# Query softmax halves and weight residuals moved from VectorE to GpSimd, key maxima written as pairwise maxima, and key maxima and stores placed later

## The chip, the cores and the metric

The kernel runs on one core of one Trainium2 chip. The metric is the time of one execution on the device in microseconds (us). The kernel before was run three times: 1423.19 us is the median, 1422.28 the lowest and 1428.6 the highest.

Names of engines in the profile: PE is TensorE's matmul, PEld its weight load, DVE is VectorE, ACT is ScalarE, POOL is GpSimd, SP is SyncE. SPq, ACTq and so on are the sequencers of those engines, which issue DMAs and waits.

## What is computed

Three layers in a row, all on 4608 tokens of width 512, with the inputs q and k scaled up. First an attention with separate softmaxes, per batch (8) and head (8), sequence 576, head width 64:

```python
q_s = softmax(q, axis=-1)        # each query over its 64 columns
k_s = softmax(k, axis=2)         # each key column over the 576 positions
kv = einsum('bhsd,bhse->bhde', k_s, v)
x = einsum('bhsd,bhde->bhse', q_s, kv)
```

Its output, as rows of 512, goes through `leaky(x @ w_in) @ w_out` (512 to 2048 to 512, slope 0.01) and then through `max(x @ w1, x @ w2, x @ w3) @ w_out` (512 to 768 to 512). The weights are 64-bit floats, the rest is 32-bit. The kernel keeps every operand of the large products as a high and a low part and adds three products (high by high, high by low, low by high).

## The kernel before, in words

**Chunks and blocks.** The 4608 tokens are 9 chunks of 512. The first layer's weights are 16 blocks `m` of 128 columns, each with its part of `w_in` and of `w_out`. A step of the first stage takes one block for one chunk: `project` (12 matmuls of 512 columns, line 622), ACT's leaky activation (L899), the split of the result into `ghi` (ACT, L642) and `glo` (DVE, L643), and, one step later, `a_out` (12 matmuls). The list `TURNS` says which chunk takes which blocks: chunks 0 and 1 take turns while the weights still arrive, 32 steps in all, then chunk 2 takes all 16 blocks in steps 32 to 47. Chunks 3 to 8 go in three pairs through a seven-product scheme of half-size blocks (L849), and the last layer follows in the same manner for eight chunks and plainly for one.

**The opening.** For chunks 0 and 1 the attention is done before their first step. `q_unit` takes a maximum over groups of 64 (L521, DVE), subtracts it (L531, DVE), takes the exponential (L532, ACT), sums (L534, DVE), and multiplies by the reciprocal (L540, DVE); PE transposes the result (L546) and multiplies it by the key-value product (L554). `kv_unit` for these two blocks takes the key maxima through PE transposes (L409, L414 to L434) and multiplies keys by values on PE (L450).

**Conversion of a weight block.** `conv_a` and `split_words` turn a block of 64-bit words into the high and low parts: ACT copies one element of the newest `g` into the work tile `ca` (L171, which ties the conversion to a step) and takes absolute values (L172); DVE does five integer and scaling operations (L173, L174, L175, L178, L179), adds (L184), and subtracts the high part, which ACT has written meanwhile (L177), to leave the low part (L185); ACT copies the sum (L188) and its queue stores it (L189) for later use. The work tile `ca` has one buffer, so a conversion begins when the one before has let go of it. `BEGUN` gives the step at which each block's conversion is written: blocks 3 to 7 at steps 2, 3, 5, 7 and 9.

**Background units.** `background(step)` is called once a step, from step 28 to 47 twice a step, and three times in each round of a pair of chunks (each live unit advances by one `yield` a call). It advances `kv_unit` and `q_unit` of later chunks, `stage_a` (stores of a converted block, SP's queue, L679 to L686), and `sums_a` (loads two stored blocks, L694, forms sums and their parts, L230 to L239, and stores them, L705, SP's queue). For blocks from 2 on, `kv_unit` fetches keys on POOL's queue (L396), takes the key maxima on DVE (L438), has POOL take the maximum over partitions (L439), subtracts (L442), takes the exponential (L443) and multiplies (L450). `behind_step` ties the maximum to the newest `g` (L372). `post()` at the start of `background` runs what the list `posted` holds, or counts it down by one call.

**What sets the order.** The order in which each engine takes its instructions is fixed when the program is built: a scheduler orders them by readiness and by their place in the program; `pin` keeps an instruction behind everything already written for its engine. At run time each engine takes its instructions in that order.

Of the kernel before, what the change touches and what calls it, by code (L numbers as in the profile page):

```python
# [18 lines left out]
P = 128  # L19
# [20 lines left out]
AHEAD = 3  # L40

BEGUN = (0, 0, 0, 2, 3, 5, 7, 9, 11, 13, 15, 17, 19, 21, 23, 25)

# [28 lines left out]
def tile_kernel(ctx: ExitStack, tc: tile.TileContext, q, k, v, wa, wb, out):  # L72
# [82 lines left out]
    def split_words(raw, hi, lo, n, after=None, whole=None, keep=None):  # L155
# [24 lines left out]
        if whole is not None:  # L180
            af, bf = (t.rearrange("p (b n) -> p b n", n=H) for t in (af, bf))
            nc.vector.tensor_tensor(whole, af, bf, op=ALU.add)
            return
        nc.vector.tensor_tensor(af, af, bf, op=ALU.add)  # L184
        nc.vector.tensor_tensor(lo, af, hi.bitcast(F32), op=ALU.subtract)  # L185
        if keep is not None:
            copy = raw.bitcast(F32)[:, :N]
            nc.scalar.activation(copy, af[:, :N], AF.Copy)  # L188
            pin(nc.scalar.dma_start(keep, copy))  # L189

# [191 lines left out]
    def kv_unit(b, hp, early):  # L382
# [15 lines left out]
        if b < FIRST:  # L398
            nc.sync.dma_start(vt, v[b, hp])
        yield  # L400
        if b < FIRST:

# [32 lines left out]
        else:  # L435
            mx = ap.tile([P, P], F32, tag="mx", name="mx", bufs=2)
            behind_step(mx[:, 0:1])
            nc.vector.tensor_reduce(mx, ke.rearrange("p r d -> p d r"), axis=AX.X, op=ALU.max)  # L438
            nc.gpsimd.partition_all_reduce(mx, mx, P, bass_isa.ReduceOp.max)  # L439
# [3 lines left out]
            nc.scalar.activation(ke, ke, AF.Exp)  # L443
            yield
        yield
# [49 lines left out]
    def q_unit(c, hp, early):  # L495
# [28 lines left out]
        if by_scalar:  # L524
            for g in range(G):
                nc.scalar.activation(
                    groups[:, g], groups[:, g], AF.Exp, bias=mx[:, g : g + 1], accum_out=sm[:, g : g + 1]
                )
            yield
        else:  # L530
            nc.vector.tensor_tensor(groups, groups, mx[:, :, None].to_broadcast([P, G, W]), op=ALU.subtract)  # L531
            nc.scalar.activation(qt, qt, AF.Exp)  # L532
            yield
            nc.vector.tensor_reduce(sm, groups, axis=AX.X, op=ALU.add)  # L534
# [4 lines left out]
        nc.vector.reciprocal(sm, sm)  # L539
        nc.vector.tensor_tensor(groups, groups, sm[:, :, None].to_broadcast([P, G, W]), op=ALU.mult)  # L540
        yield
# [147 lines left out]
    def sums_a(t):  # L689
# [9 lines left out]
        hi, lo = split_sums(room)  # L699
        yield  # L700
        i = t * len(AUSES)
        for h, z in enumerate((hi, lo)):
# [49 lines left out]
    def ahead_units():  # L752
        for m in range(MA):
            yield max(BEGUN[m] + 5, 8), stage_a(m)
        for t in range(MA // 2):
            yield (30, 34, 38, 42, 49, 53, 57, 61)[t], sums_a(t)
        for u, at in enumerate((68, 78, 88, 98, 107, 112, 115, 119, 123)):
# [600 lines left out]
```

## Time and profile before

| what | value |
|---|---|
| median of three runs | 1423.19 us (1422.28 to 1428.6) |
| the profiled execution's own time | 1424.57 us |
| its span, first to last instruction | 1422.8 us |
| mean granted TensorE clock | 0.995 |
| PE busy | 1388.7 us, 98% of the span |
| DVE busy | 874.5 us, 61% |
| ACT busy | 673.8 us, 47% |
| POOL busy | 159.9 us, 11% |

How to read it: the span is the profiled execution alone, from the first instruction to the last; its own time lies 1.77 us above the span and 1.38 us above the median of the runs. Busy time of an engine is the time in which at least one of its instructions ran; PE's matmuls are pipelined, so a busy PE is not PE at its peak.

### The profile page before, as it was taken

The numbers are of one execution on the slowest core, as the hardware profiler recorded it, in microseconds if no ns is written. First come the engines' busy times: TensorE is split into PE (matmuls) and PEld (weight loads), VectorE is DVE, ScalarE is ACT, GpSimd is POOL, SyncE is SP. The second block draws the span as 40 slices with busy tenths as digits, with TensorE's granted clock in tenths as the row PEclk, the third lists the DMA queues.
The fourth block names the chain that finished last, engine by engine and source line by source line (L and its number), as shares of the span: only waits on it lengthen the run. The fifth ranks groups of instructions, "written<-read, shape, count | busy, mean of one in ns | idle before, by whom it ended". The sixth has DMA issues, their size and how long they took to land.

```text
span 1422.8 us, 18234 instructions
## 1 busy us (share of the span) xinstructions
PE 1388.7 (98%) x6624; PEld 1130.2 (79%) x6624; DVE 874.5 (61%) x1428; ACT 673.8 (47%) x1382; POOL 159.9 (11%) x261
## 2 busy tenths in 40 slices
PE   6999999999999999999999999999999999999998
PEld 5688877788788787888887888888888888888887
DVE  8888978875686794665755636767357345434311
ACT  6756867663666654654544444334124223323211
POOL 1000212200111120210122310101000000000000
PEclk9999999999999999999999999999999999999999
DMA  9468776734877856769589897764574573464611
GB/s 372 158 246 293 260 249 204 237 124 151 326 258 274 348 178 227 258 237 359 201 312 318 308 360 267 255 232 172 187 293 166 200 283 131 140 245 155 223 36 38
DMA packets 90825, 330.09 MB, mean 232 GB/s; under 512 B 10672, under 2 KB 27056, under 8 KB 67568
## 3 DMA queue, kind: packets, MB, share of 16 engines
q1 hardware_dynamic: 68512, 251.46, 48.5%
q0 software_dynamic: 19056, 66.98, 14.0%
q10 hardware_dynamic: 3168, 10.49, 1.8%
q8 instruction: 52, 0.85, 0.2%
q14 instruction: 37, 0.30, 0.1%
HBM read 253.66 MB, written 75.24 MB: 231 GB/s over the span
## 4 chain that ended last, share of the span: by engine, by line
PE 80%; DVE 7%; DMA 5%; issue 3%; ACT 3%; POOL 0%; SPq 0%; DVEq 0%; ACTq 0%; POOLq 0%
PE ps L849 37%; PE acc L622 30%; PE ps L622 11%; DMA stream<-room 2%; PE ps L450 1%; PE ps L574 1%; DMA room<-wi 1%; DVE glo L643 1%; DMA stream_in<-room 1%; DMA spare<-in_q_dram 1%; DVE qmx L521 0%; DMA ke<-in_k_dram 0%; DMA room<-in_wb_dram 0%; DMA qt<-in_q_dram 0%; DVE side L814 0%
## 5 line engine op out<-in xcount | busy, mean ns | idle before, releaser
L849 PE MATMUL ps<-op,group 128*128 128x512 f32 x1512 | 352.2, 389 | 0.0
L849 PEld LDWEIGHTS ps<-op,group 128*128 128x128 f32 x1512 | 283.7, 188 | 59.1 <-ACT snap L1081 0.2
L622 PE MATMUL acc<-ghi,outw 128*128 128x512 f32 x768 | 250.9, 394 | 3.6 <-ACT ghi L642 3.2
L849 PE MATMUL ps<-opA,group 128*128 128x512 f32 x1008 | 249.7, 391 | 1.4 <-ACT snap L977 1.2
L849 PEld LDWEIGHTS ps<-opA,group 128*128 128x128 f32 x1008 | 188.4, 188 | 41.9 <-ACT snap L977 2.0
L622 PEld LDWEIGHTS acc<-ghi,outw 128*128 128x128 f32 x768 | 144.3, 189 | 35.6 <-ACT ghi L642 5.2
L622 PE MATMUL acc<-glo,outw 128*128 128x512 f32 x384 | 151.6, 395 | 3.7 <-DVE glo L643 3.4
L622 PE MATMUL acc<-wo,h 128*128 128x512 f32 x558 | 135.6, 389 | 0.0
L622 PE MATMUL acc<-ghi,w 128*128 128x512 f32 x384 | 127.3, 395 | 0.0
L622 PE MATMUL ps<-xhi,w 128*128 128x512 f32 x384 | 125.8, 394 | 1.2 <-ACT g L899 0.8
L1081 ACT ACTIVATE snap<-ps 128x512 f32<-128x512 f32 x108 | 61.9, 596 | 136.0 <-PE ps L849 135.7
L622 PEld LDWEIGHTS acc<-wo,h 128*128 128x128 f32 x558 | 104.7, 188 | 21.7
L1096 DVE TENSOR_TENSOR snap<-snap,ps 128x512 f32<-128x512 f32 x72 | 49.1, 684 | 93.6 <-ACT snap L1081 70.3
L643 DVE TENSOR_TENSOR glo<-g,ghi 128x512 fp32r<-128x512 f32 x102 | 69.4, 687 | 46.8 <-ACT ghi L642 46.4
L622 PEld LDWEIGHTS acc<-glo,outw 128*128 128x128 f32 x384 | 72.5, 189 | 21.4 <-DVE glo L643 6.4
L622 PEld LDWEIGHTS ps<-xhi,w 128*128 128x128 f32 x384 | 72.0, 188 | 17.7 <-ACT g L899 1.2
L642 ACT ACTIVATE ghi<-g 128x512 fp32r<-128x512 f32 x102 | 63.5, 630 | 44.2 <-DVE g L1281 27.3
L622 PEld LDWEIGHTS acc<-ghi,w 128*128 128x128 f32 x384 | 71.5, 188 | 15.8 <-ACT ghi L642 0.4
L1092 DVE TENSOR_TENSOR best<-snap,ps 128x512 f32<-128x512 f32 x36 | 24.7, 686 | 87.9 <-PE ps L849 39.1
L622 PE MATMUL acc<-glo,w 128*128 128x512 f32 x192 | 75.9, 395 | 1.8 <-DVE glo L643 1.8
L622 PE MATMUL ps<-xlo,w 128*128 128x512 f32 x192 | 75.2, 392 | 0.1
L1105 ACT ACTIVATE h<-best 128x512 fp32r<-128x512 f32 x48 | 30.3, 631 | 86.7 <-DVE best L1098 86.2
(184 smaller groups left out, 1925.3 us busy)
## 6 DMA issues: line engine op xcount, KB each, us to landing
group<-stream SPq DMA_DIRECT2D x62, 1024.0 KB, 6.6
outw<-stream_out SPq DMA_DIRECT2D x48, 1024.0 KB, 7.7
group<-stream_in SPq DMA_DIRECT2D x42, 1024.0 KB, 7.4
stream<-room POOLq DMA_DIRECT2D x66, 256.0 KB, 6.5
raw<-in_wa_dram SPq DMA_DIRECT2D x16, 1024.0 KB, 7.6
x<-st SPq DMA_DIRECT2D x40, 256.0 KB, 3.6
room<-in_wb_dram POOLq DMA_DIRECT2D x18, 512.0 KB, 5.7
stream_out<-w SPq DMA_DIRECT2D x16, 512.0 KB, 3.5
```

The costliest lines, as they stand in the source:

```text
L450: nc.tensor.matmul(acc[z, : D + 1], lhsT=ke[:, r, z], rhs=vt[:, r, h], start=r == 0, stop=r == RK - 1)
L574: nc.tensor.matmul(both(xps, c0, c1), lhsT=a, rhs=halves(y, c0, c1), start=i == 0, stop=i == 2)
L622: nc.tensor.matmul(acc, lhsT=l, rhs=r, start=first and i == 0, stop=last and i == 2)
L642: nc.scalar.activation(hi[:, z], g[:, z], AF.Copy)
L643: nc.vector.tensor_tensor(lo[:, z], g[:, z], hi[:, z].bitcast(F32), op=ALU.subtract)
L849: nc.tensor.matmul(bank, lhsT=l, rhs=r, start=fresh and first, stop=last, skip_group_check=not fresh)
L1081: nc.scalar.activation(t, bank, AF.Copy)
L1092: nc.vector.tensor_tensor(g, snap, bank, op=ALU.add)
L1096: nc.vector.tensor_tensor(snap, snap, bank, op=ALU.add)
L1105: nc.scalar.activation(h[:, m, 0], g, AF.Copy)
```

## The change: what it does, and the diff

- In `split_words`, for weight blocks 3 to 7 (those with `FIRST < len(tiles) < FIRST_MAXIMUM`), the addition of L184 runs on GpSimd, and the last part (the subtraction of L185, pinned, ACT's copy L188 and the store L189) is posted and written one step later.
- In `kv_unit` the key maxima of L438 become four `tensor_tensor` maxima of 128x128 blocks in a row.
- In `kv_unit` for blocks 5 to 7 the maxima come one background call later; a `yield` behind the exponential goes, so that the product stays at its call.
- In `q_unit` of chunks 0 and 1 the subtraction (L531) and the multiplication (L540) run on GpSimd.
- In `sums_a` the stores come one call later, and the last four of the eight units begin one step earlier. `stage_a` begins two steps later, though not before step 8.

```diff
--- before.py
+++ after.py
@@ -39,6 +39,7 @@
 PARTS = ("a11", "a12", "a21", "a22", "s2", "s4", "s1", "s3")
 AHEAD = 3
 
+FIRST_MAXIMUM = 8
 BEGUN = (0, 0, 0, 2, 3, 5, 7, 9, 11, 13, 15, 17, 19, 21, 23, 25)
 
 
@@ -181,12 +182,22 @@
             af, bf = (t.rearrange("p (b n) -> p b n", n=H) for t in (af, bf))
             nc.vector.tensor_tensor(whole, af, bf, op=ALU.add)
             return
-        nc.vector.tensor_tensor(af, af, bf, op=ALU.add)
-        nc.vector.tensor_tensor(lo, af, hi.bitcast(F32), op=ALU.subtract)
-        if keep is not None:
-            copy = raw.bitcast(F32)[:, :N]
-            nc.scalar.activation(copy, af[:, :N], AF.Copy)
-            pin(nc.scalar.dma_start(keep, copy))
+        by_gpsimd = keep is not None and FIRST < len(tiles) < FIRST_MAXIMUM
+        (nc.gpsimd if by_gpsimd else nc.vector).tensor_tensor(af, af, bf, op=ALU.add)
+
+        def finish():
+            low_part = nc.vector.tensor_tensor(lo, af, hi.bitcast(F32), op=ALU.subtract)
+            if by_gpsimd:
+                pin(low_part)
+            if keep is not None:
+                copy = raw.bitcast(F32)[:, :N]
+                nc.scalar.activation(copy, af[:, :N], AF.Copy)
+                pin(nc.scalar.dma_start(keep, copy))
+
+        if by_gpsimd:
+            posted.append((1, finish))
+        else:
+            finish()
 
     def flat(t):
         return t.rearrange("p s n -> p (s n)")
@@ -398,6 +409,8 @@
         if b < FIRST:
             nc.sync.dma_start(vt, v[b, hp])
         yield
+        if b >= CONV + 2:
+            yield
         if b < FIRST:
 
             t4, t1 = (ps_acc.tile([P, N], F32, tag="acc", name="t") if i == b == 0 else psum() for i in range(2))
@@ -435,13 +448,16 @@
         else:
             mx = ap.tile([P, P], F32, tag="mx", name="mx", bufs=2)
             behind_step(mx[:, 0:1])
-            nc.vector.tensor_reduce(mx, ke.rearrange("p r d -> p d r"), axis=AX.X, op=ALU.max)
+            nc.vector.tensor_tensor(mx, ke[:, 0], ke[:, 1], op=ALU.max)
+            for r in range(2, RK):
+                nc.vector.tensor_tensor(mx, mx, ke[:, r], op=ALU.max)
             nc.gpsimd.partition_all_reduce(mx, mx, P, bass_isa.ReduceOp.max)
             yield
             fetch.dma_start(vt, v[b, hp])
             nc.vector.tensor_tensor(ke, ke, mx[:, None, :].to_broadcast([P, RK, P]), op=ALU.subtract)
             nc.scalar.activation(ke, ke, AF.Exp)
-            yield
+            if b < CONV + 2:
+                yield
         yield
         acc = psum()
         for r in range(RK):
@@ -528,7 +544,8 @@
                 )
             yield
         else:
-            nc.vector.tensor_tensor(groups, groups, mx[:, :, None].to_broadcast([P, G, W]), op=ALU.subtract)
+            by = nc.gpsimd if c < FIRST else nc.vector
+            by.tensor_tensor(groups, groups, mx[:, :, None].to_broadcast([P, G, W]), op=ALU.subtract)
             nc.scalar.activation(qt, qt, AF.Exp)
             yield
             nc.vector.tensor_reduce(sm, groups, axis=AX.X, op=ALU.add)
@@ -537,7 +554,8 @@
         else:
             nc.vector.scalar_tensor_tensor(sm, other(sm), EPS, sm, op0=ALU.add, op1=ALU.add)
         nc.vector.reciprocal(sm, sm)
-        nc.vector.tensor_tensor(groups, groups, sm[:, :, None].to_broadcast([P, G, W]), op=ALU.mult)
+        by = nc.gpsimd if c < FIRST else nc.vector
+        by.tensor_tensor(groups, groups, sm[:, :, None].to_broadcast([P, G, W]), op=ALU.mult)
         yield
         qf = ap.tile([P, N], F32, tag=("qf", "qhi", "qlo")[hp % 3] if early else "qf", name="qf", bufs=1)
         if early:
@@ -697,6 +715,7 @@
         sums_of_quarters(b[:, :4], b[:, 4:])
         yield
         hi, lo = split_sums(room)
+        yield
         yield
         i = t * len(AUSES)
         for h, z in enumerate((hi, lo)):
@@ -751,9 +770,9 @@
 
     def ahead_units():
         for m in range(MA):
-            yield max(BEGUN[m] + 5, 8), stage_a(m)
+            yield max(BEGUN[m] + 7, 8), stage_a(m)
         for t in range(MA // 2):
-            yield (30, 34, 38, 42, 49, 53, 57, 61)[t], sums_a(t)
+            yield (30, 34, 38, 42, 48, 52, 56, 60)[t], sums_a(t)
         for u, at in enumerate((68, 78, 88, 98, 107, 112, 115, 119, 123)):
             yield at, ahead_unit(u, at > 105)
         for t, at in enumerate((136, 145, 154)):
```

## Rows read from the trace of the kernel before

**Rows 1.** The page's part 1: busy time, share of the span and instructions.
```profile
PE 1388.7 (98%) x6624; PEld 1130.2 (79%) x6624; DVE 874.5 (61%) x1428; ACT 673.8 (47%) x1382; POOL 159.9 (11%) x261
```

**Rows 2.** Stretches: length; PE, PEld, DVE, ACT, POOL busy (x); clock; DMA share; GB/s.
```profile
0.00:28.00 28.00, 16.93 (x139) 13.36 (x140) 22.23 (x63) 16.70 (x36) 5.84 (x23) 0.88 0.96 360
28.00:57.00 29.00, 25.63 (x182) 16.95 (x180) 26.46 (x61) 25.51 (x52) 0.00 (x0) 1.00 0.47 186
...
57.00:200.00 143.00, 142.96 (x701) 116.89 (x702) 121.02 (x154) 98.55 (x221) 11.88 (x16) 1.00 0.76 267
200.00:216.00 16.00, 13.14 (x54) 9.24 (x53) 12.88 (x17) 6.93 (x13) 2.15 (x2) 1.00 0.50 163
216.00:300.00 84.00, 80.07 (x484) 62.78 (x483) 72.11 (x150) 60.73 (x162) 18.30 (x31) 1.00 0.67 221
```

**Rows 3.** In order of time, DVE then PE, near 488 us: start us, us, [idle before].
```profile
488.65 1.24 DVE L438 TENSOR_REDUCE mx<-ke 128x128 f32<-128x640 f32 x1 [3.79 <-DMA ke<-in_k_dram]
...
490.42 0.88 DVE L643 TENSOR_TENSOR glo<-right,ghi 128x512 fp32r<-128x512 f32 x1
...
491.35 0.50 PE L622 MATMUL acc<-glo,outw 128*128 128x512 f32 x1 [3.18 <-DVE glo L643]
```

**Rows 4.** The chain that ended last, opening: start us, us, what.
```profile
13.04 0.61 DVE spare L531
...
29.90 0.60 DVE spare L531
...
31.69 1.20 DVE spare L531 x2
...
34.08 0.60 DVE spare L531
...
39.85 0.56 DVE spare L540
```

**Rows 5.** Instructions in order of time, ACT, beginnings of two conversions.
```profile
67.51 0.20 ACT L171 ACTIVATE ca<-g 128x1 f32<-128x1 f32 x1 [1.71 <-DVE w L185]
...
97.28 0.20 ACT L171 ACTIVATE ca<-g 128x1 f32<-128x1 f32 x1 [1.29 <-DVE w L185]
```

**Rows 6.** Instructions in order of time, the last conversion's end.
```profile
206.67 1.28 DVE L438 TENSOR_REDUCE mx<-ke 128x128 f32<-128x640 f32 x1
...
208.05 1.59 POOL L439 PARTITION_ALL_REDUCE mx<-mx  x1 [8.62 <-DVE mx L438]
...
209.13 0.30 PEld L622 LDWEIGHTS ps<-xhi,w 128*128 128x128 f32 x2 [0.63 <-DVE w L185]
```

**Rows 7.** Groups by form, DVE: form xcount | busy us, mean ns | idle before.
```profile
L438 DVE TENSOR_REDUCE mx<-ke 128x128 f32<-128x640 f32 x24 | 31.0, 1292 | 3.9 <-DMA ke<-in_k_dram 3.8
...
L531 DVE TENSOR_TENSOR spare<-spare,qmx 128x512 f32<-128x512 f32 x8 | 5.4, 683 | 0.0
...
L540 DVE TENSOR_TENSOR spare<-spare,qsm 128x512 f32<-128x512 f32 x8 | 5.3, 675 | 0.0
...
L615 DVE TENSOR_TENSOR kvlo<-plain,kvhi 128x128 fp32r<-128x128 f32 x4 | 1.1, 285 | 0.3 <-ACT kvhi L614 0.3
```

**Rows 8.** Groups by form, POOL.
```profile
L354 POOL MEMSET plain<- 128x1024 f32 x1 | 0.9, 950 | 0.0
```

**Rows 9.** Instructions in order of time, DVE, end of one conversion.
```profile
94.09 1.23 DVE L184 TENSOR_TENSOR ca<-ca,raw 128x1024 f32<-128x1024 f32 x1
95.42 0.69 DVE L643 TENSOR_TENSOR glo<-g,ghi 128x512 fp32r<-128x512 f32 x1
96.03 1.22 DVE L185 TENSOR_TENSOR w<-ca,w 128x1024 fp32r<-128x1024 f32 x1
```

**Rows 10.** Stretch behind it, columns as in rows 2.
```profile
492.00:496.00 4.00, 4.00 (x29) 2.90 (x27) 3.92 (x8) 1.37 (x2) 0.00 (x0) 0.57 0.26 72
```

**Rows 11.** Waits of SP's queue and of DVE: total us, times, longest.
```profile
SPq L705 <- ACT hi L238: 21.1, 4, 6.8
...
DVE room L230 <- DMA room<-wi: 2.0, 4, 0.8
```

## The prediction

> **What bounds the kernel now.** I read the page first, then busy time by stretches, then the chain of waits of the opening, then the instructions in order of time at the places where PE stands idle. PE is busy for 1388.7 of 1422.8 us [rows 1], so no change of this kind can give back more than 34.1 us. The stretches say where the idle time lies: 11.07 us of the first 28, 3.37 us from 28 to 57, almost none from 57 to 200, 2.86 us from 200 to 216 and 3.93 us from 216 to 300 [rows 2]. One more gap of 3.18 us stands at 488 us [rows 3].
>
> Three places matter. First, the opening: from 28 to 57 us DVE is busy for 26.46 of 29.00 us [rows 2], and the chain that ended last runs through DVE's softmax operations [rows 4]. Second, the conversions of the weight blocks. They share one work tile, so each begins when DVE's L185 of the one before is done: ACT waits for just that [rows 5]. Three of them take 97.28 - 67.51 = 29.8 us, 9.9 us each, and the row goes on to the last block, for which PE itself waits [rows 6]. So this chain, rather than PE, has the least slack from 57 to 209 us. Third, at 488 us DVE stands for 3.79 us at a key maximum whose keys have not landed; the split of the next operand is queued behind it, and PE waits for that split [rows 3].
>
> **The change, part by part.**
>
> *A. Query softmax on GpSimd.* 16 operations of about 0.68 us leave DVE, eight L531 and eight L540 [rows 7]. On the chain, four L531 for chunk 1 and one for chunk 0 take 0.61 + 0.60 + 1.20 + 0.60 = 3.01 us, and one L540 takes 0.56 us [rows 4], together 3.57 us. No row shows POOL adding two tiles. The nearest shows it filling 128x1024 in 0.95 us [rows 8], one stream. Three streams at that pace, two in and one out, are 2.85 us for 1024 columns and 1.43 us for 512; one stream is 0.48 us for 512. I take two streams, the middle: 1.90 us and 0.95 us. POOL does nothing from 28 to 57 us and works for 11.88 of the next 143 us [rows 2], so nothing on its queue is pushed back, and eight operations of chunk 1, 7.6 us, fit while DVE does the maxima and sums between; what stays on the chain is a longer hop into and out of POOL. I take -3.0 us. PE's own idle time in that stretch, 3.37 us, says nearly the same. Ends: +1 (1.43 us each, 11.4 us in a row, more than DVE had) and -5 (all eight at 0.6 us each, and a little of the 11.07 us ahead).
>
> *B. Residuals of five weight blocks.* L184 leaves DVE. From its start to the next operation's it holds DVE for 95.42 - 94.09 = 1.33 us, and before L185 DVE still does a split L643 of 96.03 - 95.42 = 0.61 us [rows 9]. On POOL it is 1.90 us and two hops: DVE to POOL 208.05 - 207.95 = 0.10 us [rows 6], and some 0.04 us back. In that time DVE can do the split. The chain then grows by 1.90 + 0.14 - 1.33 - 0.61 = +0.10 us for a block, 0.5 us for five. L185 is pinned behind what is written up to the next step, which DVE has reached by then, since conversions run behind their steps; L188 and its store L189 come later too, and their data are first read from step 30 on. Behind the waiting L185 on DVE are the next splits, for which PE waits; before it ACT's L171 of the next block. Ends: 0.95 us on POOL would shorten the chain by 0.85 us a block, but no more than the 2.86 us of idle time at its end [rows 2] can come back; 2.85 us on POOL with the split done after it gives 5 x (2.85 + 0.14 - 1.33) = +8.3 us.
>
> The Trainium skill (GPSIMD Engine Reference, Performance versus the Vector engine) speaks against this part: it gives 4.497 us for a two-input addition of 2048 columns, against 2.293 us on VectorE, and blames the shared read port. An estimate from that page for 1024 columns is 2.25 us, with which B would be +2.3 us and my sum 1417.1 us. No row here shows it.
>
> *C. Key maxima on pairs.* 24 reductions of 1.292 us become 4 operations each. The nearest is L615, two operands of 128x128, 0.285 us [rows 7]: 1.14 us for four, 0.15 us less. That counts where PE waits for DVE, which is 200 to 300 us [rows 2], with eight of the 24. Half of 8 x 0.15 us: -0.5 us. Ends: +1 (each waits for the one before) and -3 (all 24 with the ends overlapped).
>
> *D. Later key maxima, blocks 5 to 7.* Of all 24 maxima the one at 488 us alone waited for its DMA: 3.8 us [rows 3, 7]. One call later, the maximum is tied to the next pair's first activation and comes behind the landing. Back come PE's 3.18 us [rows 3] and the clock: the granted clock in the next 4.00 us was 0.57, the 1.2 GHz level for most of it, after PE had stood idle [rows 10], which is 4.00 x (1 - 0.57) = 1.72 us. Together -4.9 us. POOL's maximum, the subtraction and the exponential move with it, and the product on PE has one call less behind them; the fetch of the values does not wait for them. Late next would be that product. Ends: 0 (the wait turns up elsewhere) and -5.3.
>
> *E. Later stores.* SP's queue was held for 21.1 us by stores waiting for ACT, and DVE waited for 2.0 us in all for loads queued there [rows 11]. Stores placed later hold SP less, but the next unit's room comes free later. I take 0; ends +2 and -2. The stores of `stage_a` are hidden by the stretch from 57 to 200 us, where PE is full [rows 2]; without that cover they belong to the same ends.
>
> **The sum.** -3.0 + 0.5 - 0.5 - 4.9 + 0 = -7.9 us. The profiled execution took 1424.57 us, so 1416.7 us; it was 1.38 us above the median of 1423.19, against which this is **1415.3 us**.
>
> **The rivals.**
>
> *R1, slower: GpSimd holds the conversions.* If the addition takes 2.85 us and keeps DVE's splits waiting, the chain to 209 us grows by 8.3 us. PE is full before that, but the last block is waited for [rows 6], so the growth shows there, and a gap of that size costs the clock as at 488 us, 1.7 us. The opening gains nothing at 1.43 us an operation. With C and D: 1423.2 + 8.3 + 1.7 - 0.5 - 4.9 = 1427.8 us. It is slower than before once 5 x (a + 0.14 - 1.33) exceeds 5.4 us, from an addition `a` of 2.3 us on. For it: the row of conversions without a gap [rows 5]. Against it: the one stream that POOL shows, 0.95 us, is shorter than DVE's addition of the same width, 1.23 us [rows 8, 9].
> The Trainium skill (SBUF — State Buffer, Who interferes with whom) has a rule to this effect: a VectorE instruction with two SBUF inputs and a GpSimd instruction that reads SBUF shut one another out. No row here has both at once.
>
> *R2, the opening is held by loads and PE.* The DMA engines are busy for 0.96 of the first 28 us, and PE for 25.63 of the next 29 [rows 2]. Then A is 0: 1423.2 + 0.5 - 0.5 - 4.9 = 1418.3 us.
>
> *R3, the wait at 488 us comes back.* Another operation at the head of DVE's queue waits for a landing, since the order of all engines is made anew. Then D is 0: 1423.2 - 3.0 = 1420.2 us.
>
> *R4, more comes back.* A short addition and a DVE with room: A -5, B -2.9, C -3, D -5.3 give 1407 us.
>
> **How the numbers follow.** The forecast has 0.40, R1 0.16, R2 0.17, R3 0.13, R4 0.14. 0.5% is 7.1 us, about what a measurement can tell here: faster begins at 1416.1 us, slower at 1430.3. Faster: R4, four fifths of the forecast, which stands close to that line, and a little of R2, 0.49. Slower: half of R1, where the addition is longer still or PE starves twice, 0.08. The same: 0.43. The range from 1405 to 1426 us holds the forecast, R2, R3, most of R4 and the near side of R1; what is left out is 0.15 to 0.2.
>
> **What would show it.** A: L531 and L540 of `spare` on POOL, at about 0.95 us, and the stretch in which PE is full begins some 3 us earlier than at 57 us. B: L184 on POOL at 1.9 us for five blocks, L171 still 9.9 to 10 us apart; 11.5 us apart is R1. C: L438 with 96 operations near 0.28 us. D: no wait of L438 for a DMA, no half clock near 490 us. E: less of L705 in SP's waits. I am wrong if L171's spacing grows by over 1 us, or if PE's idle time from 200 to 300 us grows.

## The result: slower by 9 us, and the profile after

The changed kernel takes 1433.27 us (median; 1431.68 to 1434.99), the kernel before 1423.17 us beside it. The ratio is 1.0064, with a 95% interval of 1.0046 to 1.0082, so the change costs about 9 us (0.0064 x 1423) and the forecast of 1415.3 us is wrong. The profiled execution of the changed kernel took 1431.68 us, its span is 1429.9 us.

The page's part 1 of the changed kernel, for [rows 1]:

```profile
PE 1387.7 (97%) x6624; PEld 1130.3 (79%) x6624; DVE 858.9 (60%) x1479; ACT 673.3 (47%) x1382; POOL 189.2 (13%) x282
```

PE does the same work in a longer span. DVE lost 15.6 us of work and POOL took on 29.3: what moved is longer on POOL. The same stretches as [rows 2], and one more (columns: length; PE, PEld, DVE, ACT, POOL busy; clock; DMA share; GB/s):

```profile
0.00:28.00 28.00, 13.82 (x71) 10.67 (x72) 15.19 (x42) 12.96 (x26) 13.98 (x31) 0.74 0.95 355
28.00:57.00 29.00, 23.74 (x232) 17.80 (x230) 22.25 (x56) 20.77 (x46) 9.19 (x8) 0.90 0.49 192
57.00:200.00 143.00, 138.22 (x648) 109.17 (x649) 109.78 (x151) 94.42 (x205) 22.22 (x18) 1.00 0.69 237
...
216.00:300.00 84.00, 74.18 (x431) 58.03 (x432) 66.27 (x157) 55.90 (x142) 18.10 (x28) 0.98 0.63 211
460.00:580.00 120.00, 118.80 (x625) 96.54 (x624) 87.36 (x169) 72.07 (x159) 21.01 (x31) 1.00 0.70 262
```

The last of these stretches in the kernel before:

```profile
460.00:580.00 120.00, 114.54 (x553) 91.79 (x552) 82.01 (x140) 66.13 (x146) 17.84 (x25) 0.97 0.67 250
```

The time is lost ahead of 300 us and partly won back behind 460. From 57 to 200 us PE stands idle for 4.78 us (0.04 before), from 216 to 300 us for 9.82 (3.93 before). From 460 to 580 us it is busy for 4.26 us more, at the full clock: the stall at 488 us is gone, as is the half clock behind it [rows 3, 10].

Two places make the loss. The first is the opening. The view of line L548 (L531 before) gives the shortest, median and longest operation in ns, and the first and last start in us; under it stand POOL's instructions in order of time:

```profile
L548 POOL TENSOR_TENSOR spare<-spare,qmx x8: 1032/1035/2018, 17.1 to 40.3; 128x512 f32<-128x512 f32 x8
L548 POOLq MODIFY_POOL_CONFIG  x2: 44/44/44, 6.4 to 6.5; - x2
```

```profile
5.84 0.54 POOL L516 DMA_DIRECT2D qt<-in_q_dram  x1
17.13 4.04 POOL L548 TENSOR_TENSOR spare<-spare,qmx 128x512 f32<-128x512 f32 x4 [10.75 <-DMA spare<-in_v_dram]
```

VectorE began the same subtraction in the kernel before at 5.63 us, and the maximum that it needs is ready in the changed kernel too, at 4.30 + 0.69 = 4.99 us (DVE, before and then after):

```profile
5.63 0.68 DVE L531 TENSOR_TENSOR spare<-spare,qmx 128x512 f32<-128x512 f32 x1
```

```profile
4.30 0.69 DVE L537 TENSOR_REDUCE qmx<-spare 128x8 f32<-128x512 f32 x1 [0.47 <-DMA spare<-in_q_dram]
```

On GpSimd two short instructions, MODIFY_POOL_CONFIG, stand ahead of the subtraction at 6.4 us, and it starts at 17.13. The kernel before has the same two at 6.4 us, but there the instruction behind them, a maximum over partitions (L439), starts only at 132.6 us. The first matmul that uses a weight block in step 1, PE's first row behind the opening, moves by 8.4 us, here before and then after:

```profile
55.77 0.50 PE L622 MATMUL ps<-xhi,w 128*128 128x512 f32 x1 [0.22 <-DVE xlo L606]
```

```profile
64.16 0.50 PE L640 MATMUL ps<-xhi,w 128*128 128x512 f32 x1 [0.57 <-DVE xlo L624]
```

The second place is the row of conversions. ACT's L172 (L171 before) begins one, and 35.27 us instead of 29.8 pass from the first to the fourth, 11.8 us each [rows 5]. In order of time, ACT, with POOL and DVE in one of them:

```profile
75.55 0.20 ACT L172 ACTIVATE ca<-g 128x1 f32<-128x1 f32 x1 [1.71 <-DVE w L189]
...
82.49 2.43 POOL L186 TENSOR_TENSOR ca<-ca,raw 128x1024 f32<-128x1024 f32 x1 [36.19 <-ACT g L918]
...
82.64 2.83 DVE L661 TENSOR_TENSOR glo<-g,ghi 128x512 fp32r<-128x512 f32 x1 [0.28 <-ACT ghi L660]
85.39 1.21 DVE L189 TENSOR_TENSOR w<-ca,w 128x1024 fp32r<-128x1024 f32 x1
...
84.95 0.63 ACT L194 ACTIVATE raw<-ca 128x512 f32<-128x512 f32 x1 [2.34 <-POOL ca L186]
...
86.64 0.20 ACT L172 ACTIVATE ca<-g 128x1 f32<-128x1 f32 x1 [1.05 <-DVE w L189]
...
110.82 0.20 ACT L172 ACTIVATE ca<-g 128x1 f32<-128x1 f32 x1 [0.63 <-DVE w L189]
```

The addition takes 2.43 us, and DVE's split beside it 2.83 instead of 0.69: it ends 0.55 us after POOL does. ACT's copy L194 waits for POOL, and the next conversion's L172 is queued behind that copy; but the copy is done at 85.58 us, and L172 waits on for DVE's low part L189, which ends at 86.60. So it goes in four of the five conversions: L172 begins 0.03 us after the low part and 0.6 to 1.05 us after the copy. In the fifth, at 98.68 us, ACT was still busy with work behind an activation (L918) that had waited 2.33 us for a split beside POOL's addition. By the first matmul of step 47 (335.93 us before, 353.61 after) 17.7 us are lost; 7.1 remain at the end of the span.

### The profile page after: what moved, and what is told of

The parts are those of the page before. It is cut to its first block, busy times and chain, and to the rows that moved or that the text cites. A ratio compares the mean times of both kernels' runs of the same rounds, so it can differ in the third digit from the quotient of the medians.

```text
span 1429.9 us, 18358 instructions
## 1 busy us (share of the span) xinstructions
PE 1387.7 (97%) x6624; PEld 1130.3 (79%) x6624; DVE 858.9 (60%) x1479; ACT 673.3 (47%) x1382; POOL 189.2 (13%) x282
## 4 chain that ended last, share of the span: by engine, by line
PE 84%; DVE 7%; ACT 5%; DMA 2%; issue 2%; POOL 0%; SPq 0%; ACTq 0%; DVEq 0%; POOLq 0%
PE ps L868 39%; PE acc L640 32%; PE ps L640 10%; DVE glo L661 1%; PE ps L592 1%; PE ps L466 1%; DMA spare<-in_v_dram 1%; ACT g L918 1%; ACT ghi L660 1%; ACT qo L530 0%; DMA room<-wi 0%; DMA stream_in<-room 0%; DVE ca L186 0%; DVE raw L180 0%; DVE side L833 0%
## 5 line engine op out<-in xcount | busy, mean ns | idle before, releaser
L640 PE MATMUL acc<-ghi,outw 128*128 128x512 f32 x768 | 247.9, 391 | 1.4 <-ACT ghi L660 1.0
L661 DVE TENSOR_TENSOR glo<-g,ghi 128x512 fp32r<-128x512 f32 x102 | 74.0, 732 | 59.2 <-ACT ghi L660 58.6
L660 ACT ACTIVATE ghi<-g 128x512 fp32r<-128x512 f32 x102 | 63.4, 629 | 39.5 <-DVE g L1300 27.3
```

What stands on the lines that cost most here:

```text
L640: nc.tensor.matmul(acc, lhsT=l, rhs=r, start=first and i == 0, stop=last and i == 2)
L660: nc.scalar.activation(hi[:, z], g[:, z], AF.Copy)
L661: nc.vector.tensor_tensor(lo[:, z], g[:, z], hi[:, z].bitcast(F32), op=ALU.subtract)
```

## The experiments

All 16 kernels compute what the changed kernel computes. A is the subtraction and the multiplication of the query softmax on GpSimd, B the five residual additions on GpSimd, C the maxima on pairs, D the later maxima, E the later stores. Times are medians in us; the kernel before ran beside them each time, at 1422.5 to 1425.3.

| kernel | what it has | time | ratio to before, 95% interval |
|---|---|---|---|
| changed | A B C D E | 1433.3 | 1.0064, 1.0046 to 1.0082 |
| e1 | the same, first GpSimd addition at the head | 1428.5 | 1.0040, 1.0023 to 1.0056 |
| e2 | B C D E | 1427.2 | 1.0012, 0.9998 to 1.0027 |
| e3 | A C D E | 1425.0 | 1.0002, 0.9991 to 1.0013 |
| e4 | C D E | 1418.3 | 0.9952, 0.9935 to 0.9970 |
| e5 | A for chunk 1 only, C D E | 1413.3 | 0.9926, 0.9910 to 0.9942 |
| e6 | C D E and B's order, on VectorE | 1417.8 | 0.9959, 0.9944 to 0.9974 |
| e7 | B without its order, C D E | 1428.1 | 1.0027, 1.0014 to 1.0041 |
| e8 | C E | 1425.6 | 1.0016, 1.0004 to 1.0028 |
| e9 | D E | 1422.1 | 0.9997, 0.9987 to 1.0007 |
| e10 | C D | 1417.9 | 0.9968, 0.9956 to 0.9980 |
| e11 | e5 and chunk 0's products on GpSimd | 1415.5 | 0.9953, 0.9939 to 0.9966 |
| e12 | e5 without E | 1413.1 | 0.9938, 0.9924 to 0.9952 |
| e13 | e6 and spare additions on GpSimd | 1429.4 | 1.0038, 1.0024 to 1.0051 |
| e14 | e4, C for blocks 5 to 7 only | 1415.0 | 0.9931, 0.9918 to 0.9943 |
| e15 | e5, C for blocks 5 to 7 only | 1411.7 | 0.9904, 0.9891 to 0.9917 |
| e16 | e6 and spare additions that nobody waits for | 1418.2 | 0.9949, 0.9929 to 0.9969 |

The parts A and B add up: from e4, A costs 1.0002 - 0.9952 = 0.50% (7.1 us) and B 1.0012 - 0.9952 = 0.60% (8.5 us); with the 6.8 us that C, D and E give, that is +8.8 us, and the change measures +9.1.

### e1: the first addition at the head of GpSimd's work

Against the changed kernel:

```diff
+    first_add = const.tile([P, 1], F32, name="first")
+    nc.gpsimd.memset(first_add, 0.0)
+    nc.gpsimd.tensor_tensor(first_add, first_add, first_add, op=ALU.add)
     ones = const.tile([P, P], F32, name="ones")
```

> The changed kernel with one tiny GpSimd add (128x1) put at the head of GpSimd's work, so that whatever a first tensor_tensor costs on GpSimd is paid before the loads fill the DMA engines; the computation is unchanged. Theory 1 (the opening is lost to the 10.7 us between GpSimd's last DMA issue, 6.4 us, and its first add, 17.1 us, in which its code is loaded): the first L551 (was L548) starts at 5 to 9 us, the first project matmul of step 1 comes at 54 to 57 us instead of 64.2, and the time falls by 6 to 9 us, to 1424 to 1427. Theory 2 (the opening is lost because sixteen adds and multiplications take 1.04 to 1.16 us on GpSimd instead of 0.68 on VectorE, and hold up VectorE's small instructions): the first project matmul stays at 62 us or later and the time at 1430 to 1434. In either case the conversions of weight blocks 3 to 7 stay 10.7 to 11.2 us apart.

Neither theory's numbers: the first L551 starts at 15.12 us, the first project matmul comes at 65.4 us, and yet the time falls by 3.4 us (1.0064 to 1.0040; the two intervals overlap). POOL in order of time says why the opening stays:

```profile
0.90 0.20 POOL L135 MEMSET kvhi<- 128x128 f32 x1
9.46 0.18 POOL L126 TENSOR_TENSOR first<-first 128x1 f32<-128x1 f32 x1 [8.36 <-issue]
9.60 0.19 POOL L135 MEMSET kvlo<- 128x128 f32 x1
...
15.12 4.04 POOL L551 TENSOR_TENSOR spare<-spare,qmx 128x512 f32<-128x512 f32 x4
```

The addition of 128x1 waits for no data and still comes 8.36 us late: this is a cost of the first addition as such, whoever asks for it. At the head it pushed back POOL's fills, of which VectorE needs one, and the five DMA issues of POOL's queue, behind which L551 stands. VectorE's whole opening stood behind that fill (DVE's waits):

```profile
DVE kvhi L139 <- POOL kvhi L135: 8.1, 1, 8.1
```

So the cost of a first addition is shown; I call it the load of GpSimd's code, after the MODIFY_POOL_CONFIG ahead of it. That the opening is lost to it isn't shown by this run. Where its 3.4 us come from is open.

### e2 to e4: A undone, B undone, both undone

```diff
-            by = nc.gpsimd if c < FIRST else nc.vector
+            by = nc.vector
...
-        by = nc.gpsimd if c < FIRST else nc.vector
+        by = nc.vector
```

```diff
-FIRST_MAXIMUM = 8
+FIRST_MAXIMUM = 0
```

e2 has the first of these, e3 the second, e4 both.

> The changed kernel with the query softmax of the first two chunks back on VectorE; the five residual additions stay on GpSimd; the computation is unchanged. Theory 1 and theory 2 both expect the first project matmul of step 1 back at 55 to 57 us (before 55.8, after 64.2), since in theory 1 GpSimd's code load starts at 6.5 us all the same and is over long before the first addition at about 65 us; the time falls by 7 to 9 us, to 1424 to 1426. If the load begins only when the addition is ready, the first addition comes 6 to 10 us late and the first conversion on GpSimd takes 17 to 20 us. The conversions stay 10.7 to 11.2 us apart.

The first project matmul is back at 56.85 us, the conversions stay 11.6 us apart. The addition isn't late: MODIFY_POOL_CONFIG stands at 6.4 us here too and the first addition comes at 75.5, so the code's load is hidden. The time, 1427.2 us, is 1.2 us above the range.

> The changed kernel with the five weight blocks' residual additions back on VectorE; the softmax stays on GpSimd; the computation is unchanged. Theory: the 128x1024 addition takes 2.43 us on GpSimd instead of 1.23 on VectorE, and VectorE's splits (glo) wait it out, up to 2.8 us instead of 0.69, which makes the conversions 10.7 to 11.2 us apart instead of 9.9; undone, they are 9.4 to 10 us apart, conversion 7 ends 7 to 9 us earlier than 132.7 us (124 to 126), the first project matmul stays at 64 us, step 17 comes at 142 to 145 us instead of 150.9, and the time falls by 5 to 8 us, to 1425 to 1428. Rival: the conversions follow the loads and the matmuls, which the late opening has moved, and not the additions: then conversion 7 still ends at 130 us or later and the time stays at 1431 to 1434.

The theory holds: L172 comes every 9.9 us again, conversion 7 ends at 123.6 us (0.4 us before the range), step 17 at 142.6, the first project matmul stays at 63.4 us, and the time is 1425.0 us.

> The changed kernel with both GpSimd parts undone: only the key maxima on pairs, the later key maxima and the later stores are left; the computation is unchanged. If the two GpSimd parts are all of the loss, step 1's first project matmul is back at 55.8 us, no matmul waits near 490 us, and the time is the kernel before less 4 to 9 us: 1414 to 1419, under both kernels. Rival: the 10.6 us that the changed kernel gains back after 353 us were slack given by its late opening and not by the moved maxima: then the time is 1421 to 1424, as before.

1418.3 us, as expected: A and B are all of the loss, and the rest of the change is a gain of 0.48%, faster than both kernels.

### e5 and e11: which chunk's softmax costs

e5, against e3:

```diff
-            by = nc.gpsimd if c < FIRST else nc.vector
+            by = nc.gpsimd if 0 < c < FIRST else nc.vector
...
-        by = nc.gpsimd if c < FIRST else nc.vector
+        by = nc.gpsimd if 0 < c < FIRST else nc.vector
```

> As e3 (residual additions on VectorE), but GpSimd does the subtraction and the multiplication only for the second chunk's query softmax, the first chunk's are VectorE's again; the computation is unchanged. Theory 1 (the opening is lost to the loading of GpSimd's code, 10.7 us, and the first chunk waits for it): the load from 6.4 us now lies beside the first chunk's work on VectorE, the first project matmul of step 1 comes at 54 to 57 us and the time is that of e4, 1416 to 1420. Theory 2 (the adds' length of 1.04 us and what they hold up on VectorE): eight of the sixteen operations are left, so a third to a half of the loss of 7 us (e3 against e4) stays: first project matmul at 58 to 61 us, time 1420.5 to 1423.

1413.3 us. Theory 1 holds, and more: with the code's load beside the first chunk (GpSimd's first operation comes at 28.9 us), A costs nothing and gives 0.26% (3.7 us) over e4, at the same 1.04 us for a typical operation. e11 puts the first chunk's products, which come later than its subtractions, on GpSimd as well (the second of the two lines as in the changed kernel).

> As e5 (GpSimd does the second chunk's softmax operations), and the first chunk's four multiplications on GpSimd too, which come when its code has been loading since 6.4 us for 8 us or more; the computation is unchanged. Theory 1 (only the load costs): the first multiplication starts at 16.5 to 18 us as VectorE's did, and the time is e5's within 1.5 us, 1412 to 1415, or less. Theory 2 (the operations' length costs wherever the opening waits for them): four of the eight operations in the first chunk at 1.04 us instead of 0.68 and their holds on VectorE, 1.5 to 4 us more than e5, 1415 to 1418.

```profile
5.73 0.55 POOL L516 DMA_DIRECT2D qt<-in_q_dram  x1
17.06 4.04 POOL L558 TENSOR_TENSOR spare<-spare,qsm 128x512 f32<-128x512 f32 x4 [10.78 <-ACT spare L446]
```

Another operation, in another place of the computation, and again the first one starts at 17.1 us, 10.8 us after the last DMA issue. The releaser named in brackets is another one each time (a DMA in the changed kernel, ACT here, none in e1), so none of them explains all three, and the DMA's last piece lands only at 17.21 us in the changed kernel and at 17.73 in e3, behind the first subtraction (17.13 and 16.34). The reciprocal that the first product needs was ready at 14.98 us. VectorE did the first of these products at 16.3 us in the kernel before, so little is late: the first project matmul comes at 57.8 us (e5 57.5). The median is 2.2 us above e5's and 2.4 above e12's of the same group, with intervals that overlap e12's; it lies 0.5 us above theory 1's range and just inside theory 2's, so a cost of up to 2 or 3 us for four operations isn't excluded. e3 differs from e11 by the first chunk's four subtractions alone, and takes 0.49% more (1.0002 - 0.9953), 7.0 us: what costs is the subtractions that had to wait for the load.

### e6, e7, e13 and e16: what of B costs

e6 against e2, with B's order but not its engine:

```diff
-        (nc.gpsimd if by_gpsimd else nc.vector).tensor_tensor(af, af, bf, op=ALU.add)
+        nc.vector.tensor_tensor(af, af, bf, op=ALU.add)
```

> As e2 (softmax on VectorE), and the five residual additions on VectorE too, but the low part and the copy that follow each still come one turn later; the computation is unchanged. Theory L (the loss of e2 against e4, 8.9 us, is the GpSimd addition's 2.43 us for 1.23 and the splits that wait behind it): with the order alone left, the conversions of blocks 3 to 7 are 9.4 to 10.2 us apart and the time is 1417 to 1421. Rival O (the loss is the turn by which the low part is put off, whatever engine adds): the conversions stay 10.5 to 11 us apart and the time 1425 to 1428.

e7 against e2, with the engine but not the order:

```diff
-        if by_gpsimd:
-            posted.append((1, finish))
-        else:
-            finish()
+        finish()
```

> As e2 (softmax on VectorE, five residual additions on GpSimd), but the low part follows in VectorE's order at once and not a turn later, so that VectorE waits out the GpSimd addition; the computation is unchanged. Theory L: the length and the hold of the addition are still all there, and VectorE now stands still for them: conversions 10.5 to 12 us apart, time 1426 to 1431. Rival O: without the turn's delay most of the loss goes: conversions 9.8 to 10.3 us apart, time 1418 to 1422.

The order costs nothing (1417.8 us, L172 9.9 us apart), the engine everything (1428.1 us, 11.6 us apart). Length or hold? e13 against e6 puts an addition beside the splits:

```diff
         nc.vector.tensor_tensor(af, af, bf, op=ALU.add)
+        if by_gpsimd:
+            nc.gpsimd.tensor_tensor(bf, bf, bf, op=ALU.add)
```

> As e6 (residual additions on VectorE, the low part a turn later), and after each of the five additions GpSimd does one addition of the same 128x1024 shape whose result nobody uses (it overwrites the block's spent high words); of what is computed nothing is changed. No conversion waits for the length of GpSimd's addition; it only lies beside VectorE's splits. Theory H (the hold): VectorE's split (glo) and the low part, which read two operands, stand still while GpSimd adds, 2 to 3 us instead of 0.69 as in the changed kernel, and that alone makes the conversions late: 10.2 to 11 us apart, first project matmul of step 17 at 139 us or later (e6 135.8), time 1421 to 1427. Theory N (the length alone: 2.43 us in the chain for 1.23): the conversions stay 9.4 to 10 us apart and the time 1416 to 1420.

1429.4 us, even over theory H's range (the profiled execution was the fastest, 1423.2 us). But something did wait, ACT's copy of the block's first half into the words that GpSimd overwrites. ACT, in order of time:

```profile
102.83 0.63 ACT L196 ACTIVATE raw<-ca 128x512 f32<-128x512 f32 x1 [5.66 <-POOL raw L188]
103.50 0.33 ACTq L197 DMA_DIRECT2D wi<-raw  x1
103.87 0.20 ACT L172 ACTIVATE ca<-g 128x1 f32<-128x1 f32 x1 [0.40 <-ACT raw L196]
```

The next conversion sits behind that copy: in four of the five, L172 begins 0.40 us after the copy and 2.82 us after the low part, and the conversions are 12.4 us apart. So e16 takes only words that the copy leaves alone:

```diff
-            nc.gpsimd.tensor_tensor(bf, bf, bf, op=ALU.add)
+            spent = bf[:, N // 2 :]
+            nc.gpsimd.tensor_tensor(spent, spent, spent, op=ALU.add)
```

> As e13, but GpSimd's spare addition covers only 768 of the 1024 high words, those that ScalarE's copy does not overwrite (in e13 ScalarE's copy L196 waited 19.4 us for the spare additions, and the next conversion is queued behind it); now nothing at all waits for GpSimd's additions, which lie beside VectorE's work; of what is computed nothing is changed. Theory H (the hold alone makes the loss): VectorE's splits and low parts that meet an addition still take 1.5 to 2.5 us, the conversions stay over 10.3 us apart and the time is 1421 to 1427. Theory Q (the loss is what queues behind the addition: VectorE's low part, and ScalarE's copy with the next conversion behind it): single splits are held, but the conversions are 9.4 to 10.2 us apart, the first project matmul of step 17 comes at 135 to 138 us and the time is 1416.5 to 1420.5.

DVE and then POOL in order of time, the third and the fourth of the five:

```profile
97.86 2.49 DVE L192 TENSOR_TENSOR w<-ca,w 128x1024 fp32r<-128x1024 f32 x1
...
107.88 1.23 DVE L192 TENSOR_TENSOR w<-ca,w 128x1024 fp32r<-128x1024 f32 x1
109.03 1.96 DVE L664 TENSOR_TENSOR glo<-g,ghi 128x512 fp32r<-128x512 f32 x1
...
97.48 1.79 POOL L189 TENSOR_TENSOR raw<-raw 128x768 f32<-128x768 f32 x1 [9.12 <-DVE ca L186]
107.98 2.45 POOL L189 TENSOR_TENSOR raw<-raw 128x768 f32<-128x768 f32 x1 [8.71 <-DVE ca L186]
```

In the first three conversions the hold is all there (the low part takes 2.49 us instead of 1.22 and ends 1.08 us after POOL), 1.27 us each, and the spacing grows to 10.8 us, as theory H had it. In the last two the low part comes first and is not held, 1.23 us; POOL's addition takes 2.45 us instead of 1.79, the split behind the low part is held, and the spacing is 8.8 us and 9.5 us. Step 17 comes at 137.1 us (e6 135.8), and the time, 1418.2 us, is e6's. So the hold, on the low part in three of five conversions, costs 1.3 us by step 17 and nothing that the end shows. The loss needs something that waits for POOL: in e13 it is ACT's copy, in e2 and the changed kernel that copy and VectorE's low part. Waits of the changed kernel from 57 to 140 us (total us, times, longest):

```profile
ACT raw L194 <- POOL ca L186: 10.6, 3, 4.3
...
DVE w L189 <- POOL ca L186: 5.7, 2, 3.0
ACT g L918 <- DVE glo L661: 5.1, 4, 2.3
ACT ca L172 <- DVE w L189: 4.5, 5, 1.7
```

The copy waits longest, but what L172 waits for last is the low part, as shown above; so e13's loss is of its own making and does not explain the changed kernel's. Summed from L172 to L172 over the five conversions, e2 takes 58.8 us and e6 49.2. Of the 9.6 us between them 6.0 are the addition itself (12.1 against 6.1), 0.8 lie ahead of it, 0.8 between it and the low part, and 2.0 between the low part and the next L172. So the larger part is the addition's length in a chain that waits for it, the cause that theory N named and e13 could not test. How the other 3.6 us divide between the hold and ACT's and DVE's order was not tried.

### e8 to e10, e12, e14 and e15: C, D and E

Against e4, e8 takes out D's two edits, e9 takes the maxima by one reduction again, e10 takes out E's three edits; e12 is e10's edit on e5.

> As e4 (neither GpSimd part), and the key maxima of blocks 5 to 7 at their old place; left are the maxima on pairs of blocks and the later stores; the computation is unchanged. If the later maxima are the gain, as the prediction's sum has it (4.9 of 5.4 us), the wait near 490 us and its half clock are back (PE busy 114 to 115.5 us of 460 to 580) and the time is 1421.5 to 1424. Rival: the gain comes from the maxima on pairs or the later stores: the time stays at 1417 to 1420.

> As e4 (neither GpSimd part), with the key maxima taken again by one reduction over the five blocks instead of four maxima on pairs; left are the later maxima and the later stores; the computation is unchanged. Theory P (the prediction's term C, -0.5 us): 0 to 2 us slower than e4, 1418 to 1421. Rival: e8 showed that the maxima on pairs and the later stores together cost about 2 us, and it is the four instructions that cost it: then 1415.5 to 1417.5.

> As e4 (neither GpSimd part), with the stores of the weight blocks, the sums and their stores at their old places; left are the maxima on pairs and the later maxima; the computation is unchanged. Theory P (the prediction's term E, 0): the same as e4 within 1 us, 1417 to 1420. Rival: the 2 us that e8 lost beside the kernel before are the moved stores and sums, whose wait of SyncE on the sums' high parts grew from 21 to 33 us between 216 and 300 us and with it the matmuls' wait from 3.9 to 6.5 us: then 1414 to 1417, with 2 to 3 us less PE idle time between 216 and 300 us.

> As e5, with the stores of the weight blocks, the sums and their stores at their old places as in e10; the computation is unchanged. If what e10 shows against e4 adds to e5: by theory P the same as e5, 1412 to 1415; by the rival 2 to 3 us less, 1410 to 1412.

e10 and e12 say that E costs and gives nothing beyond the scatter, as forecast. e8 and e9, both 1 to 2 us above their ranges, were a surprise: without D the kernel is 0.16% slower than before, without C it is as fast as before, and together they give 0.4%. PE's stretches (e8, then e9, then e4; columns as above):

```profile
216.00:300.00 84.00, 77.57 (x469) 61.71 (x468) 66.80 (x165) 59.32 (x159) 17.61 (x30) 0.96 0.64 211
460.00:580.00 120.00, 115.77 (x569) 92.08 (x568) 80.98 (x152) 67.19 (x148) 18.23 (x27) 0.97 0.69 252
```

```profile
216.00:300.00 84.00, 80.98 (x490) 63.94 (x489) 72.69 (x150) 60.86 (x162) 18.27 (x31) 1.00 0.69 224
460.00:580.00 120.00, 115.18 (x563) 92.34 (x562) 84.50 (x144) 69.54 (x152) 19.36 (x30) 0.99 0.70 261
```

```profile
216.00:300.00 84.00, 77.47 (x470) 61.70 (x470) 67.03 (x167) 59.73 (x159) 17.60 (x30) 0.96 0.65 215
460.00:580.00 120.00, 118.76 (x610) 97.04 (x609) 86.90 (x166) 72.79 (x160) 22.45 (x32) 1.00 0.74 276
```

With either part alone PE still stands for 4 to 5 us of the later stretch: in e8 at 492 us, as before, in e9 at 480, 504 and 538 us, with a half clock behind the last. Only both clear it. And C has a price at the other end, 3.5 us of PE between 216 and 300 us (77.5 against 81.0), mostly one wait for ACT's split at 235 us, 4.2 us long; behind it, from 240 to 244 us, the granted clock is 0.50. Since the later stretch has key blocks 5 to 7 alone, C can be limited to them:

```diff
-            nc.vector.tensor_tensor(mx, ke[:, 0], ke[:, 1], op=ALU.max)
-            for r in range(2, RK):
-                nc.vector.tensor_tensor(mx, mx, ke[:, r], op=ALU.max)
+            if b < CONV + 2:
+                nc.vector.tensor_reduce(mx, ke.rearrange("p r d -> p d r"), axis=AX.X, op=ALU.max)
+            else:
+                nc.vector.tensor_tensor(mx, ke[:, 0], ke[:, 1], op=ALU.max)
+                for r in range(2, RK):
+                    nc.vector.tensor_tensor(mx, mx, ke[:, r], op=ALU.max)
```

e14 has this against e4, e15 against e5.

> As e4 (neither GpSimd part), but the maxima on pairs only for key blocks 5 to 7; blocks 2 to 4 are reduced by one instruction as before; the computation is unchanged. Theory: the maxima on pairs cost 3 us between 232 and 242 us, where TensorE stands 4.2 us, and give back 4 to 5 us at 530 to 550 us, where only blocks 5 to 7 are at work; so PE is busy 80 to 81 us of 216 to 300 (e4 77.5) and still 118.5 or more of 460 to 580, and the time is 1413 to 1416. Rival: the two are one thing, the gain at 530 to 550 us comes from the order that the early pairs leave: then the time is 1417 to 1422 and the stall of 530 to 550 us is back.

> As e5 (second chunk's softmax operations on GpSimd), with the maxima on pairs only for key blocks 5 to 7; the computation is unchanged. If e5's gain over e4 (5 us) is the opening's, 2 to 3 us come on top of it: 1410 to 1412. If it is the stall at 232 to 242 us that e5 happened to shorten, nothing comes on top: 1412 to 1416.

e14's stretches:

```profile
216.00:300.00 84.00, 79.96 (x484) 62.87 (x484) 72.02 (x150) 60.30 (x162) 18.33 (x31) 1.00 0.67 219
460.00:580.00 120.00, 117.95 (x595) 96.19 (x591) 85.85 (x163) 72.38 (x159) 23.05 (x34) 1.00 0.73 271
```

The PE values are 0.04 and 0.55 us short of what was written, the time is as written, 1415.0 us. And it seems to add to the second chunk's softmax, though the intervals of e15 and e5 overlap: e15 takes 1411.7 us, 0.96% under the kernel before and the fastest of all.

## Why the prediction was wrong, step by step

Both signs that it named for being wrong came: L172's spacing grew by 1.8 us, and PE's idle time from 200 to 300 us from 6.79 to 10.91 us.

**A, forecast -3.0 us, measured +7.1.** This step failed at "nothing on its queue is pushed back ... what stays on the chain is a longer hop". POOL's queue was free, but POOL couldn't add yet: its first two-operand instruction starts 8.4 us (e1), 10.0 us (e3) or 10.8 us (changed kernel, e11) after it is asked for, and chunk 0's four subtractions waited for that. I costed POOL's work by a fill of 0.95 us, which needs no such load, and gave the start no price. The length was taken well (0.95 us forecast, 1.04 measured), and where the load is hidden the gain is near what I forecast: -3.7 us (e5 against e4, with intervals that just overlap; e15 against e14 0.27%, 3.8 us, with intervals that don't). But its place is not the one I named, so that the number agrees is luck as far as the runs show. The first project matmul of step 1 isn't earlier: it comes at 57.5 us in e5 (e4 55.9), whose profiled execution began PE's work 1.5 us late (5.26 us against 3.79), and at 56.35 us in both e15 and e14, which began alike. The lead is there by step 28 (e5 212.6 against e4 213.9; e15 211.4 against e14 214.4) and larger at step 47 (334.4 against 339.1; 331.9 against 336.5). Why is not settled; the new order of all engines is a rival that no run excludes.

The Trainium skill (GPSIMD Engine Reference, Instruction dispatch) says that the first call into freshly loaded code pays about 6 us of loading with no instruction to show for it. This case's traces agree in kind and show more, 8.4 to 10.8 us. The DMA share was 0.92 over e1's wait and 1.05 over the changed kernel's; what sets the length no run shows.

**B, forecast +0.5 us, measured +8.5.** Two terms failed. The addition takes 2.43 us, not 1.90 (+0.53 us a block, 2.7 us in all), and "In that time DVE can do the split" is false: the split stood still beside it, 2.83 us for 0.69, so the 0.61 us a block that the sum took off for it (3 us in all) was not saved. With both put right the prediction's own sum gives 5 x (2.43 + 0.14 - 1.33) = +6.2 us. The rest, some 2 us, it had no term for; in e2 the next L172 begins 2.0 us in all later behind the low part than in e6. The path was right: each conversion waits for the low part of the one before. That L188's copy (L194 now) "comes later too" left out the next conversion, queued behind it on ACT, but in the changed kernel the copy was not what released it: in four of the five conversions the low part ended later. e6 and e7 show that the engine costs and not the order, e16 that the hold is the smaller part.

The estimate of 2.25 us that the prediction drew from the Trainium skill (GPSIMD Engine Reference, Performance versus the Vector engine) was nearer than its own 1.90: 2.43 us measured, 1.98 times VectorE's 1.23.

R1 had this case: 11.5 us between conversions was its sign (11.8 measured), the chain was to grow by 8.3 us (B costs 8.5), and its point of decision, an addition of over 2.3 us, was passed. Its time of 1427.8 us is e2's, 1427.2, but partly by luck: it took 2.85 us for the addition, and at the measured 2.43 its formula gives 6.2 us, not 8.3. It fell short of the changed kernel by the load that no rival had. The trace also bears out the rule of the Trainium skill cited with it (SBUF — State Buffer, Who interferes with whom), that a VectorE instruction with two operands and GpSimd shut one another out (2.83, 2.27 and 2.49 us beside GpSimd, 0.69 and 1.22 alone).

**C, D and E, forecast -5.4 us, measured -6.8** (e4). The sum came near by luck, since its parts were wrong. D alone gives nothing: the wait at 488 us does come back elsewhere without C, which is what R3 said. C alone costs 2 us (e8, with E, which costs nothing): the shorter maxima I priced at -0.5 us changed the order of all engines, for worse near 235 us, and for better near 540. In the changed kernel the sign of D was seen as forecast, no wait of a key maximum and no half clock near 490 us. E was right.

**R2**, in which A is worth nothing, is out: half of A gives 3.7 us (e5). What it said of the opening is not out, since step 1 began no earlier in e15 than in e14. **R4** is out as well.

## What to carry to other kernels

Before moving work to an engine, look in the trace for whether that engine has done such an instruction by then: here the first one started 8 to 11 us late, and only work that came later than that gained. A moved instruction costs its own length on the new engine where a chain waits for its result, here through VectorE's low part with the next block behind it; of several waits for it, the one that ends last counts, and not the longest. And edits that each remove one stall of a chain need not add: undo them one at a time and in pairs before keeping or dropping one.

## What the runs showed of the hardware that was not expected

- GpSimd's first two-operand instruction starts 8.4 to 10.8 us after it is asked for, with two short instructions of 44 ns or less ahead of it and nothing else in the trace; a 128x1 addition pays it as a 128x512 one does.
- Two-operand instructions of VectorE stand still while GpSimd adds, and end 0.55 us (128x512) to 1.08 us (128x1024) after GpSimd. So does a tiny one with a single operand: in the changed kernel VectorE's L553 over 128x8 takes up to 1.10 us beside GpSimd and ends within 0.04 us of the GpSimd instruction that it met, against 0.16 us for the same operation (L536) in the kernel before, where GpSimd was idle. It is mutual: in e16 an addition that met VectorE's low part already at work took 2.45 us, against 1.79.

VectorE in order of time in the changed kernel's opening, where GpSimd's instructions end at 21.17, 22.18 and 23.18 us (the first row met only the last 0.14 us of one), and then in the kernel before:

```profile
21.03 0.18 DVE L553 TENSOR_SCALAR qsm<-qsm 128x8 f32<-128x8 f32 x1
...
22.10 1.10 DVE L553 TENSOR_SCALAR qsm<-qsm 128x8 f32<-128x8 f32 x1
```

```profile
15.62 0.16 DVE L536 TENSOR_SCALAR qsm<-qsm 128x8 f32<-128x8 f32 x1
```
